# Part of a softmax's row maxima moved from one VectorE reduction per key block to a relu on ScalarE and one fused VectorE pass per two blocks

## The chip, the core and the metric

One of the eight cores of a Trainium2 chip runs the whole kernel. The metric is device time in microseconds (us), the median of a few executions. Beside it stands one execution recorded by the hardware profiler, which gives the start and length of each engine's instructions. The engines are TensorE (PE, with its weight loads as PEld), VectorE (DVE), ScalarE (ACT), GpSimd (POOL) and SyncE (SP, which here issues the DMA transfers). Each works through its own instructions in order and waits on the others only where data or buffers demand it.

## The reference

A block of a transformer in fp32: layer norm, attention with 32 query heads that share one key and one value head, a residual, a second norm, and a feed-forward part with a gated relu.

```python
B, S, D, H = 1, 2048, 512, 32          # Dh = D // H = 16, F = 1792
q = (x @ wq).reshape(B, S, H, Dh).transpose(0, 2, 1, 3)
k = x @ wk
v = x @ wv
scores = einsum("bhqd,bkd->bhqk", q, k) * (Dh ** -0.5)
p = softmax(scores, axis=-1)
o = einsum("bhqk,bkd->bhqd", p, v)
return o.transpose(0, 2, 1, 3).reshape(B, S, H * Dh) @ wo
...
gate = einsum("bsd,df->bsf", x, W_gate)
up = einsum("bsd,df->bsf", x, W_up)
h = gate * (gate > 0) * up
return einsum("bsf,fd->bsd", h, W_down)
...
h = x + A(layernorm(x))
h2 = h + B(layernorm(h))
```

The softmax needs, for each of the 32 heads and each of the 2048 queries, the maximum of 2048 scores. The change is about how these maxima are formed.

## The kernel before

**Precision.** Matmuls run in fp32r, a rounded fp32. Where more is needed, an operand is kept as a rounded part and a remainder, and a product is made of three matmuls (`PASSES`, line 262). GpSimd makes most of these splits: `split_sb` (lines 237 to 241) rounds with a `tensor_scalar` and subtracts with a `tensor_tensor`.

**Units.** The queries are cut into 8 tiles of 256 tokens, and each tile's attention into 4 units of 8 heads: 32 units (`UNITS`). For a unit the queries of its heads lie in one of three buffers `qaug`, the keys of all 2048 tokens in `kaug`. Both hold two copies, in partitions 0 to 63 and 64 to 127; a matmul uses one copy (64 rows of the array), so TensorE runs two lanes beside each other. Letters in lower case mean the lower lane, capitals the upper.

**The maxima (M, m).** `max_mm` (line 612) makes one matmul of 128 queries against a block of 512 keys into a PSUM bank (line 620), and VectorE reduces it to one column of the tile `mpart` (line 622). A unit has 32 steps in each lane: four key blocks j, two halves p, four groups c of 128 queries. `max_finish` (line 624) takes the maximum over the four blocks, splits it, transposes it and sends it through DRAM (`c_dram`) into two further rows of the unit's `qaug`, where it is subtracted by the next matmul.

**The scores (E, e).** `score_mm` (line 653) multiplies 128 keys with 512 queries (line 659); ScalarE takes the exponential out of the bank into a tile `p` (line 662).

**The value blocks (O).** `value_block` (line 666) multiplies the exponentials of 128 keys with the values (line 675), in a bank of its own, "O". All 128 rows are used, so both lanes pause. There are 512 of them, 16 for each unit. `unit_out` (line 690) carries a unit's output away, divides it by its sums on GpSimd and splits it.

**The chains (G, g).** Projections and feed-forward products are chains of matmuls, each in a lower and an upper half (`Chain.half`, line 290, issued at line 297): queries, the output projection of a tile (`front`, line 812), gate and up (`gate_up`, line 853), and down (line 893). When the upper half of a gate chain ends, `hidden` (line 857) issues a relu and a copy on ScalarE (862, 868), the product on GpSimd (870), and then, on GpSimd as well, the splits of the gate and up weights two steps ahead, of the hidden values, and of a down weight, eight instructions. The last tile's gate and up run after all else with the whole array (line 288).

**Banks.** Seven PSUM banks, B0 to B6, go round among maxima, scores, chains and transposes. A bank comes free when VectorE or ScalarE has read it.

**The order.** From line 1033 on, a planner keeps a clock for each lane and engine. What is issued next is written out by hand: `ORDER` is a row of 11,274 letters, and the loop from line 1174 takes one at a time; T stands for transposes and whole matmuls in the first part. `starts` (lines 1209 to 1232) says for each kind when it could start, and the branches from line 1260 issue it and move the planner's clocks with the constants of lines 38 to 42 (`EXP` 494, `RED` 600 ns and so on). These clocks decide when deferred work (splits, loads, residuals) is placed between the letters; instructions go to the engines in the order in which the code issues them. Maxima of a unit may start as soon as its queries are loaded (`qtime`), which needs the scores of the unit three before to be done, and at most one unit ahead of the last finished one.

**Setup.** Key block t comes from `kv(t)` (line 476): `kvt` holds the block unrounded, `kaug` the rounded copy, and its remainder rows are subtracted on VectorE or, for t of 2 and 3, on GpSimd (line 498). The rows of x lie in tiles `xs`: the first 512 tokens in two of the eight `p` tiles, the second in `h`, the third in four tiles `x`, the fourth in four tiles `xn`; later `front` uses two of the `x` and two of the `xn` tiles for each tile of 256 tokens.

Of the kernel before, what the change touches and what calls it, by code (L numbers as in the profile page):

```python
# [8 lines left out]
F32 = mybir.dt.float32  # L9
# [30 lines left out]
EXP, EXP_FREE, RED, RED_FREE, COPY, ADD, FREE = 494, 650, 600, 740, 541, 600, 150  # L40
ROUND, DIFF, PRODUCT, SCALE, HOP, ISSUE = 640, 1290, 1150, 640, 2600, 600
# [8 lines left out]
    "TTTTMMMmMMmmmmmMmTMMmTTTTTMgMggMgmgggMgMggmgmgTTmmTTGmGmGTgMgMgGgMgGGgGgGmggGgGgGGgTTMgMmgGgMGggGgGgMgGgMGmGgG"  # L50
    "gGmgGGmGggGgGgGgGGmMgTmMgGgGgMgGgGGgGmGmGggGgGgMgGgGgGgMGmgGMgGggMGmGGgGggGmGGgGgGmgGgMgGMgGgGmggmGGgGgGggGgMg"
    "MgGgGgMGmGgGmgGgGmGGgGgGmGgGgMgGgGgGgGgGgGgGgMmGgGgGgGgGgGgMgGgGgGgMgGgGmGmGgGgGgGgGmGmMgEgGgGgEgGgMgEgeGGmeGG"
    "mGeGGmGmGmOMeeMeGgGGggMEggMeGgMgEgMgGgEmGGgmMOmEEgmMOMeeGGmeGeGGmeGGmGmGmOmEEgMgEgGggMgEgMgEgMgEgGgGmMmOEmeGeG"
    "GmeGGmGgGgEgMeGgGmEgGgMeGgMgEgGgMgMmOgMeEmMOmEeGmGeGeGGmGgGgMgEgGmEgGmGgGmeGMmOMeEgEgMgOmEmEMeOmEEgMmOeMeMMgOM"
    "geEmMOeMeGGmeGeGGmGeGmGgGgMgEgGgMgEgMgEgMggGEgGmmMOeGGmeGeGmGMmOEmeGeGGmgGGmEgGgMgEgMgEggGgMMmOeMeMgMOeMeEgMMg"
    "OEmEmmMOEmEmOEmeGGmeGeGGmGeGmGEmGeGmGGmMOEeEmMmOMEeEemMOeMmEmEOeMmEEMeOeEeMmEOEemMMeEOeMeEEmMOEeEmeMMOMeEeEmMO"
    "MeEeEMmOeMeEmMOEmEEeeMmMOMeeEEmMOmEEeeMMOMeEeEmMOMmeEeMOmEeeMEEmMOMeeEEMmOEmeEeMMOMmeEmEOMeeMEemEmOeMEmeMEOeME"
    "eEmmOeEmEMeOMEeMmeEOmMEeEmOMeMEEeeMmOEeMmeEmOMmeEEemOEmMeeEmOEmEmeeMOEmeeEmMOeMEmeMEOMemEMEeOMmmEmEeOemeMMEeEm"
    "meMOmMmEEeOMeEmEmOMeMEMmMmeeEOmEMeeMOEmmMMEeEeOmMEeEmOemmMOMmmMMmMEeEeeEMemEOmEeeMEmOMmeEeMOmEmmeeEMmOEmMeEeMm"
    "OeMeMEgEgggMEgMggEgMgMgEggMmOmEeGeGGmeGGmGgGgMgEgMgGgEgMgEgMgGggGmGeGGmmGeGOOmEeGGmeGeGmGeGmGeGGmOMmEmeMOEemEO"  # L60
    "MMeEmeOmMEMMEEeMOmEMeOEmmMmeeOMggEggMggEggMggggEggMggEgggMgOMggMggMmEgGgGgGgGgGeGGgGgEggEggGgGgGmGGeGGmGGeGGgM"
    "ggEggMggGgGgGGmMgeGEgOOmGGeGGmGGeGGmGGeGGmGeGGGMmOEmeGGGgGgMgEggMgggEggMggGgEgGmGgGMeOEmgMgEggMgEgggMgOeMGmGeG"
    "GmGGeGGmGGeGGmGGgGgGgEggGeGGmGGgGgEggMggGgMggEgGgMmOOeMEggEggMggEggMmOeMeGGmGGmGGeGGgGgEggGgMgEggGgMggEggGmGGg"
    "GeGGmGGgGeGmGGgGeMOOmEgMgEggEggMggMmOeGGeGGmGGeGmGGmGGeGGGmGOOmEEegMGgGGgGgMgEgGMgEgMgEgMgGgGmGGeGgGgGmGeGgMgE"
    "gMgEgGgGmMeGgGmEgGgGgGmeMgGggGgeGgGgmGeGgGgGmGeGggOOOEggMggEggMggEggGggMggGmEeGgGgGgGgGeGGmGGgGmGGeGGgMggEggGg"
    "GmGGeGGgGmGGeGOOOemMEggMggEggMgggEggMgOEmeGGmGGeGGgGgGgMggEggGgMgEggGmGgGeGGgMggGEmgGGggGeGGgGgMgEegGgGGgMmOOE"
    "meGGmGGeGGeGGmGGeGGmGGeGGmGGGmGOOMeEggMggEggGgGgMggEggMggEggGgMgEgggEgGMggMOmEeGGmGGeGGeGGmGGeGGmGGeGGmGGGeGGm"
    "GOmMEeGmGOmEeMOeMEgMgEgEggMgEgMgEgMgMggMOOEmeEMgGggGgGmEgGeGgMEggGmGeGgMEgGgMgGmeGGggEggGgeGgGmGgeGmGgGeGmGgmG"
    "eGgGmMgOOMeEggEggMggEgggEggMgOOgMmEeEgGgGgGgGgGgGgMmGgGgGeGgGgMgEggGmGGgGeGgGgMgEggGgGgGgGgGmGGeMeGGmGOOOmEeGG"
    "mGGeGGeGGGmGeGGmGGeGGgGgGgGmGEggGgMggEgggMggMgOOEmeEggMgMgggEggMggOmEeGGmGGeGGmGGeGGmGGeGGgGgGgGmGGeGMggGgGgEg"  # L70
    "gMggGgEggEgGgMmOOMeEggEggMggEggMmOeMmGGeGGmGeGGGmGGeGGmGGeGGmGOeMEmeGGgGGgGGMgEggMgEgEgGEgMgEgMgOOMmEegGGgGmGg"
    "eGgGGmMegGEggMgGEgGggMgGGmEegGgGggGggGmGeGmGeGggMggGmEggGeGmGgOOMemEeMOOmEMggEggMggEggMggEgOeMGmGeGGmGGeGGmGGe"
    "GGmGGeGGmGGGeGGGGmGeEOMmmEMeEOeEmMEeOEmMmEeOMmEeeMOmEMggMEgEggMMgOMeEggGMgEggEgMgGeGmGgEgMgGgGgMmEgGgGeGgEgMgG"
    "gGeGmGeGmOOOeMEggGmEGgMgMggGmGEgGgeGGggGMgmGEeOeGGmeGgGmGeGGmeGGmGemGGmeGOmEeMOEMMEMmEOeEOMemEgMggEgggMgEgggMg"
    "EgggMggEgOMeEmMgggggggMmgeGGgEggGgGgGeGGgmGGmGGgGeGGmGGeGGgGgGmGGeGGgMggEgOOMggEgggMEgggMgEgmMOeEmGGeGGgGgMggG"
    "gEggGGmGeGGgGgMggEggGmGGeGGmGGeGmGGGgeGMgOOmEeMEggEggggMggMgOmEeGGmGGeGGmGGeGGmGGeGGgGgGgMggEggGgGmGGeGMggGgEg"
    "gGgGgMgmEOOeMEggMggEggEggmMOeMeEGmGgGgGgGgGgMgEggGgGmGeGGgMgEggGgGmGeGGgGmGGeGGgGeGGmMOOmEMgEggMggEggeMgOEmeGG"
    "eGGmGGeGGmGGeGGmGGGeGGmGOOMgEggMEggGMgEgMgGgEgEgGMeGgGGmMOOEmeGGmeGeGGmGeGmGgGgMgEgGgMgEgMgEgGgMgMgGmEggGggGge"
    "GgGggGeGmGgeGmGgGeGmGgOOOOgMgEggMggEggEgMggggEmegggMggEggGmGGeGGgMggEggGmGGgGeGGgGmGGeGGmGGgGeGGmGgGeGMgOOmEMg"
    "gEgMggEggeEOeMeGGmGGGmGeGGmGGgGgGgMggEggGgMgEggGgGgGgGmGGeGgGgGmGGOOeMEggMggEggEggmMOeGGmGGeGGmGeGGmGGeGGgGgGg"  # L80
    "MggEggMggGEggMgggGEmgGgGGgeMGggGGgEmGgOMeEmMeOEmeMEggMgOOGmGeGGmGGeGGeGGmGGeGGmGGeGGmGGmEOMeEgEgMgGgGgGMgEgEgM"
    "gEgGgMgMOOEmeGmGgGMggEeGgMgEgGgMgEgGmGeGgMgEmGgGmGeGeGgGggGgMggEggGmGeGggGmGeGmGeGgGmOOOMeEggEggMggEggMggEgggM"
    "OgMgEeGmGgGGggGmGGeGMggGgGmEgGgGgGeGGgGgMgmEgGgGgGeGGmGGgGeMOOmEEegMgEggggMmOeGGeGGmGGeGGmGGeGGmGGmGGgGgGgGeGG"
    "gMggEggGgGgGgMggEggMgEggMggOOEmeMEggMggOmEeEGggMgGgGgGgGmGeGGgGgMgEggGmGeGGmGGgGeGGGgmGGeGGgGgMgmEOOMeEggMggEg"
    "MggEgOmGGeGGeGGmGGeGGmGGeGGmGOOMgEggMEggMGgEgGgGMgEgGgMgGGmGeGGmGgGgEgGgMgEgGgMeGgGmEgGeGgMgEgGmGeGGggMggGmGgm"
# [71 lines left out]
def block_kernel(ctx: ExitStack, tc: tile.TileContext, x, wq, wkv, wo, wgu, wd, out):  # L157
# [924 lines left out]
    def place(k, dep):  # L1082
        return max(lanes[k], issued, dep + LOAD)
# [267 lines left out]
```

## Time and profile before

| what | value |
|---|---|
| median of 3 runs | 1745.73 us (1745.44 to 1750.38) |
| span of the profiled execution | 1747.6 us |
| TensorE: matmul busy, count | 1729.8 us, 15,566 |
| VectorE busy, instructions | 1461.8 us, 2,535 |
| ScalarE busy, instructions | 1252.0 us, 2,487 |
| GpSimd busy, instructions | 848.7 us, 1,004 |
| moved by DMA | 144.07 MB |

Every row of a profile view has the engine, the line of the code, the operation, the output and the inputs by the program's names ("mpart<-B"), their shapes and a count. In the view by groups the numbers behind the bar are the busy time in us, the mean length of one in ns, and the idle time of the engine before them with what ended it. In the timeline a row starts with its start and its length in us, both of the merged group; in the chain of waits likewise. The chain is followed back from the last instruction: at each step to what released it, or to the instruction before it on its engine, so its shares say what set the end. A busy engine is not a limiting one: TensorE's matmuls overlap, and an interval counts once however many run in it.

In the middle of the kernel, in each 200 us, VectorE is busy for about 170 us and GpSimd for about 114:

```profile
600.00:800.00 200.00, 200.00 (x1949) 137.54 (x1943) 170.34 (x295) 146.18 (x291) 117.47 (x140) 1.00 0.27 82
1000.00:1200.00 200.00, 199.88 (x1928) 135.54 (x1927) 168.54 (x290) 145.97 (x290) 114.02 (x137) 1.00 0.27 82
```

(columns: stretch and its length, busy time and count of PE, PEld, DVE, ACT and POOL, granted clock, share and GB/s of DMA).

### The profile page before, as it was taken

How to read it: one execution, taken by the hardware profiler on the slowest of the kernel's cores; microseconds unless marked ns; L12 is line 12 of the kernel's file. 1: busy time of each engine (PE TensorE's matmuls, PEld its weight loads, DVE VectorE, ACT ScalarE, POOL GpSimd, SP SyncE). 2: the span in 40 equal slices, each digit the busy share in tenths (PEclk: the TensorE clock that was granted, in tenths of full speed). 3: DMA queues.
4: the chain of work that ended last, by engine and by line, in shares of the span. 5: the costliest groups of instructions: out<-in, count | busy, mean ns of one | idle time of the engine just before them, and what ended most of it. 6: DMA issues, size and time to landing. Idle time of an engine off the chain costs nothing.

```text
span 1747.6 us, 40171 instructions
## 1 busy us (share of the span) xinstructions
PE 1729.8 (99%) x15566; PEld 1157.3 (66%) x15566; DVE 1461.8 (84%) x2535; ACT 1252.0 (72%) x2487; POOL 848.7 (49%) x1004
## 2 busy tenths in 40 slices
PE   8999999999999999999999999999999999999999
PEld 6864344676656677667666676666667667665788
DVE  8799999888898888988888878988888888885466
ACT  7378987777777777777767767777767777778524
POOL 5422201665527656366626665357546556375510
PEclk9899999999999999999999999999999999999989
DMA  3234111322212222323222222222222223122333
GB/s 128 76 92 114 37 32 31 97 90 78 82 58 92 73 79 77 92 81 96 74 71 88 80 83 77 84 73 83 80 79 90 77 84 95 54 86 68 117 131 116
DMA packets 101970, 144.07 MB, mean 82 GB/s; under 512 B 27156, under 2 KB 39572, under 8 KB 101780
## 3 DMA queue, kind: packets, MB, share of 16 engines
q1 hardware_dynamic: 100724, 141.19, 26.5%
q8 instruction: 122, 2.00, 0.5%
q14 instruction: 68, 0.56, 0.1%
q10 hardware_dynamic: 1056, 0.33, 0.1%
HBM read 119.73 MB, written 21.49 MB: 81 GB/s over the span
## 4 chain that ended last, share of the span: by engine, by line
PE 92%; DVE 7%; DMA 1%; issue 0%; ACT 0%; SPq 0%; POOL 0%; POOLq 0%; ACTq 0%
PE B L297 28%; PE O L675 27%; PE B L620 16%; PE B L659 16%; DVE mpart L622 4%; PE B L288 4%; PE B L515 1%; PE O L927 0%; DMA qaug<-c_dram 0%; PE B L404 0%; DMA c_dram<-mturned 0%; DVE kaug L498 0%; DVE msplit L631 0%; DVE bnst L345 0%; PE B L582 0%
## 5 line engine op out<-in xcount | busy, mean ns | idle before, releaser
L622 DVE TENSOR_REDUCE mpart<-B 128x1 f32<-128x512 f32 x2048 | 1268.5, 682 | 201.0 <-PE B L620 100.4
L662 ACT ACTIVATE p<-B 128x512 f32<-128x512 f32 x2048 | 1091.4, 606 | 358.0 <-PE B L659 194.1
L620 PE MATMUL B<-kaug,qaug 62*128 62x512 f32 x2048 | 760.9, 423 | 6.0 <-DVE hT L567 2.1
L659 PE MATMUL B<-qaug,kaug 64*128 64x512 f32 x2048 | 714.0, 417 | 3.9 <-DMA qaug<-c_dram 3.0
L297 PE MATMUL B<-hn,gu 64*128 64x256 f32 x4704 | 573.8, 281 | 0.0
L297 PEld LDWEIGHTS B<-hn,gu 64*128 64x128 f32 x4704 | 541.6, 186 | 22.1 <-issue 11.6
L675 PE MATMUL O<-p,vv 128*32 128x512 f32 x4096 | 511.4, 601 | 0.0
L620 PEld LDWEIGHTS B<-kaug,qaug 62*128 62x128 f32 x2048 | 353.8, 185 | 159.6 <-DVE mpart L622 49.1
L659 PEld LDWEIGHTS B<-qaug,kaug 64*128 64x128 f32 x2048 | 338.8, 185 | 168.4 <-DVE mpart L622 57.4
L297 PE MATMUL B<-wd,hT 64*128 64x512 f32 x1176 | 273.3, 399 | 0.6 <-DVE wd L247 0.6
L240 POOL TENSOR_TENSOR gu<-wraw,gu 128x512 fp32r<-128x512 f32 x197 | 256.3, 1301 | 16.4
L870 POOL TENSOR_TENSOR hf<-hf,ga 128x256 f32<-128x256 f32 x91 | 66.9, 735 | 398.6 <-ACT hf L868 393.6
L675 PEld LDWEIGHTS O<-p,vv 128*32 128x32 f32 x4096 | 99.7, 108 | 189.8 <-issue 171.1
L297 PEld LDWEIGHTS B<-wd,hT 64*128 64x128 f32 x1176 | 192.6, 187 | 14.4 <-DVE mpart L622 1.9
L239 POOL TENSOR_SCALAR gu<-wraw 128x512 fp32r<-128x512 f32 x197 | 123.3, 626 | 20.5 <-PE B L297 19.4
L240 POOL TENSOR_TENSOR wd<-wraw,wd 128x512 fp32r<-128x512 f32 x91 | 117.5, 1291 | 7.6
L297 PE MATMUL B<-wo,act 64*128 64x512 f32 x384 | 88.5, 393 | 0.0
L725 POOL TENSOR_TENSOR raw<-raw,scale 128x512 f32<-128x512 f32 x15 | 19.3, 1289 | 141.5 <-DMA x<-x 71.6
L862 ACT ACTIVATE ga<-B 128x256 f32<-128x256 f32 x112 | 43.5, 388 | 49.6 <-PE B L288 32.2
L240 POOL TENSOR_TENSOR hT<-hf,hT 128x256 fp32r<-128x256 f32 x94 | 70.4, 749 | 7.8
L297 PEld LDWEIGHTS B<-wo,act 64*128 64x128 f32 x384 | 62.4, 185 | 4.8 <-issue 1.7
L357 POOL TENSOR_TENSOR rs<-ve,nhalf 128x2 f32<-128x2 f32 (+1 forms) x13 | 10.2, 784 | 112.0 <-DVE nm L353 111.9
(139 smaller groups left out, 932.2 us busy)
## 6 DMA issues: line engine op xcount, KB each, us to landing
wraw<-wgu SPq DMA_DIRECT2D x224, 256.0 KB
wraw<-wd SPq DMA_DIRECT2D x112, 256.0 KB
q_dram<-act SPq DMA_DIRECT2D x32, 256.0 KB
qaug<-q_dram SPq DMA_DIRECT2D x62, 128.0 KB
o_dram<-osb SPq DMA_DIRECT2D x31, 256.0 KB
x<-x SPq DMA_DIRECT2D x20, 256.0 KB
out<-h SPq DMA_DIRECT2D x16, 256.0 KB
qaug<-q_dram SPq DMA_DIRECT2D x62, 64.0 KB
```

Source lines behind the costliest of these rows:

```text
L239: nc.gpsimd.tensor_scalar(dst[:, 0], src, 1.0, 0.0, op0=ALU.mult, op1=ALU.add)
L240: nc.gpsimd.tensor_tensor(dst[:, 1], src, dst[:, 0].bitcast(F32), op=ALU.subtract)
L288: nc.tensor.matmul(out(self.bank), l(a), r(b), start=i == 0, stop=i == len(self.ops) - 1)
L297: mm = nc.tensor.matmul(out(self.bank), l(a)[rows], r(b)[rows], start=opens and which == 0, stop=closes and which == 1)
L620: nc.tensor.matmul(b, qaug[v][r, p, c * 128:(c + 1) * 128], kaug[r, j * 512:(j + 1) * 512], start=True, stop=True)
L622: nc.vector.tensor_reduce(mpart[v][:, ab, p, c, j:j + 1], b, axis=AX.X, op=ALU.max)
L659: nc.tensor.matmul(b, kaug[r, kb * 128:(kb + 1) * 128], qaug[v][r, p, :], start=True, stop=True)
L662: nc.scalar.activation(probs[g][:, ab], b, AF.Exp, scale=DH ** -0.5)
L675: nc.tensor.matmul(obank[v][32 * h:32 * h + 32], vv[:, kb, :], probs[g + p][:, ab], start=kb == 0, stop=kb == NB - 1)
L725: nc.gpsimd.tensor_tensor(raw, raw, scale, op=ALU.mult)
L862: nc.scalar.activation(ga[:, :n], p[:, :n], AF.Relu)
L870: nc.gpsimd.tensor_tensor(hf[:, :n], hf[:, :n], ga[:, :n], op=ALU.mult)
```

## The change

For two key blocks with scores a and b, max(a, b) = b + relu(a - b), and a - b is the query times the difference of the two keys. A new letter D (or d) issues the matmul with key differences `kdiff` in place of key block 2, followed by a relu on ScalarE into an SBUF tile; the next maximum in that lane, key block 3, is then reduced by one fused VectorE instruction that adds the relu's tile and takes the maximum along the row. Key block 2's column of `mpart` stays at its start value, so each unit's `mpart` is set to -3e38 first, on GpSimd. The steps of a unit's second half alternate between key blocks 2 and 3; before, block 2's eight steps in each lane came ahead of block 3's. Where no D stands, a maximum is reduced as before.

`kdiff` is made once, on GpSimd, after key block 3. Three `relu` tiles and `kdiff` take the room of four row tiles: `x` and `xn` have two buffers each now in place of four, and xs[2] lies in two more of the `p` tiles. `ORDER` is a new row: 11,268 letters, of them 976 m, 928 M, 48 d, 96 D (1,024 each of m and M before), as many e, E, g, G and O as before, 12 T (18 before).

```diff
+JOINT, APART, RELUS = 640, 2900, 3
...
+    kdiff = consts.tile([128, T], F32R, name="kdiff")
+    lows = consts.tile([128, 1], F32, name="lows")
...
+    nc.gpsimd.memset(kdiff.bitcast(F32), 0.0)
+    nc.gpsimd.memset(lows, 0.0)
+    for b in (32, 96):
+        nc.gpsimd.memset(lows[b:b + 16], -1.0)
...
     def row_tiles(tag, n=4):
-        return [sb.tile([128, D], F32, name=tag, bufs=4) for _ in range(n)]
+        return [sb.tile([128, D], F32, name=tag, bufs=2) for _ in range(n)]
...
-    xs = [[b[:, c] for b in [rows_tile(tag) for _ in range(2)] for c in range(2)] for tag in ("p", "h")]
-    xs += [row_tiles("x"), row_tiles("xn")]
+    xs = [[b[:, c] for b in [rows_tile(tag) for _ in range(2)] for c in range(2)] for tag in ("p", "h", "p")]
+    xs += [row_tiles("x", 2) + row_tiles("xn", 2)]
...
+    def apart(when):
+
+        rows = slice(0, 112)
+        nc.gpsimd.tensor_tensor(kvts[2][rows], kvts[2][rows], kvts[3][rows], op=ALU.subtract)
+        for b in (0, 64):
+            nc.gpsimd.tensor_scalar(kdiff[b:b + 48], kvts[2][b:b + 48], 1.0, 0.0, op0=ALU.mult, op1=ALU.add)
+        for b in (32, 96):
+            nc.gpsimd.tensor_tensor(kdiff[b:b + 16], kvts[2][b:b + 16], kdiff[b:b + 16].bitcast(F32), op=ALU.subtract)
+        stamp["apart"] = on("P", when, APART) + FREE
...
+                if t == 3:
+                    apart(when)
...
-    def max_mm(m, ab, tag):
-
-        v, i = divmod(m, STEPS)
-        j, p, c = i // 8, i // 4 % 2, i % 4
+    def max_step(m):
+
+        i = m % STEPS
+        if i < STEPS // 2:
+            return i // 8, i // 4 % 2, i % 4
+        return 2 + i % 2, (i - STEPS // 2) // 8, (i - STEPS // 2) // 2 % 4
...
+    def max_mm(m, ab, tag, apart=False):
+
+        v = m // STEPS
+        j, p, c = max_step(m)
         if v not in mpart:
             mpart[v] = sb.tile([128, 2, 2, 4, 4], F32, name="mpart", bufs=2)
+            nc.gpsimd.memset(mpart[v], -3e38)
         r = slice(64 * ab, 64 * ab + 62)
         b = bank(tag)
-        nc.tensor.matmul(b, qaug[v][r, p, c * 128:(c + 1) * 128], kaug[r, j * 512:(j + 1) * 512],
-                         start=True, stop=True)
-        nc.vector.tensor_reduce(mpart[v][:, ab, p, c, j:j + 1], b, axis=AX.X, op=ALU.max)
+        keys = kdiff[r] if apart else kaug[r, j * 512:(j + 1) * 512]
+        nc.tensor.matmul(b, qaug[v][r, p, c * 128:(c + 1) * 128], keys, start=True, stop=True)
+        part = mpart[v][:, ab, p, c, j:j + 1]
+        if apart:
+            relus[ab] = sb.tile([128, T], F32, name="relu", bufs=RELUS)
+            nc.scalar.activation(relus[ab], b, AF.Relu)
+        elif ab in relus:
+            over = relus.pop(ab)
+            nc.vector.tensor_tensor_reduce(out=over, in0=b, in1=over, scale=1.0, scalar=-3e38, op0=ALU.add, op1=ALU.max,
+                                           accum_out=part)
+        else:
+            nc.vector.tensor_reduce(part, b, axis=AX.X, op=ALU.max)
...
+                if max_step(w)[0] == 2 and "apart" in stamp:
+                    starts["dD"[k]] = place(k, max(qtime[w // STEPS], bfree[tag], stamp["apart"]))
...
+        elif kind == "D":
+            max_mm(me[k], k, tag, True)
+            lanes[k] = s + PASS
+            slots[k] = len(joined)
+            e0 = max(clk["A"], s + SEEN, joined.get(len(joined) - RELUS, 0.0))
+            joined[slots[k]] = 0.0
+            clk["A"] = e0 + EXP
+            bfree[tag] = e0 + EXP_FREE
+            relu_end[k] = e0 + EXP + 100
+            me[k] += 1
         elif kind == "M":
+            joint = k in relus
             max_mm(me[k], k, tag)
             lanes[k] = s + PASS
-            r0 = max(clk["V"], s + SEEN)
-            clk["V"] = r0 + RED
-            bfree[tag] = r0 + RED_FREE
+            r0 = max(clk["V"], s + SEEN, relu_end.pop(k, 0.0))
+            ns = JOINT if joint else RED
+            clk["V"] = r0 + ns
+            bfree[tag] = r0 + ns + RED_FREE - RED
+            if joint:
+                joined[slots.pop(k)] = clk["V"]
             me[k] += 1
...
```

The rest of the diff is the new row, the dictionary in which the `kvt` tiles are kept, and the planner's use of `key_of`, which names the key block that a step needs. `lows` is not read anywhere.

More of the change, by code (lines that the diff above doesn't have):

```diff
@@ L1042, in block_kernel @@
     exps, oend, qtime = {}, {}, {0: QUERIES_AT}
+    relu_end, joined, slots = {}, {}, {}
     maxed, loaded = 0, 1
@@ L1214, in block_kernel @@
             if w < N and w // STEPS in qtime and w // STEPS <= maxed + 1 and tag and (
[L1215 to L1216 removed]
+                    w >= STEPS or key_of(w) in stamp):
+                starts["mM"[k]] = place(k, max(qtime[w // STEPS], bfree[tag], stamp[key_of(w)] if w < STEPS else 0.0))
+                if max_step(w)[0] == 2 and "apart" in stamp:
+                    starts["dD"[k]] = place(k, max(qtime[w // STEPS], bfree[tag], stamp["apart"]))
             if c is not None and (c.tag or tag):
```

214 lines of the change are left out of this document (108 added, 106 removed).

## The prediction

> **What bounds the kernel now.** I read the page first, then the chain of waits as a whole and cut to two stretches, then the busy time by stretches, then single groups and pieces of the timeline.
>
> ```profile
> span 1747.6 us, 40171 instructions
> PE 1729.8 (99%) x15566; PEld 1157.3 (66%) x15566; DVE 1461.8 (84%) x2535; ACT 1252.0 (72%) x2487; POOL 848.7 (49%) x1004
> ...
> PE 92%; DVE 7%; DMA 1%; issue 0%; ACT 0%; SPq 0%; POOL 0%; POOLq 0%; ACTq 0%
> ```
>
> The last line is the chain by engine: TensorE sets the end for 92% of the span. The 99% busy share says less, since matmuls overlap. VectorE is the only other engine on the chain. The maxima's share of it (line 622) is in these rows: the whole span, the steady middle (400 to 1500 us), and the longest pieces of line 622.
>
> ```profile
> by line: PE B L297 28.1%; PE O L675 26.6%; PE B L620 15.9%; PE B L659 15.6%; DVE mpart L622 4.4%; PE B L288 3.5%; PE B L515 0.7%; PE O L927 0.5%; DMA qaug<-c_dram 0.4%; PE B L404 0.4%; issue 0.4%; DMA c_dram<-mturned 0.3%; DVE kaug L498 0.3
> by line: PE B L297 32.5%; PE O L675 29.9%; PE B L620 17.8%; PE B L659 17.0%; DVE mpart L622 1.5%; PE B L404 0.5%; DVE msplit L631 0.2%; DVE msplit L632 0.2%; issue 0.1%; DVE mfin L627 0.1%; DVE bnst L345 0.1%; DVE mturned L635 0.1%; DVE h L
> 65.67 6.66 DVE mpart L622 x11
> 72.45 13.17 DVE mpart L622 x22
> 272.89 14.38 DVE mpart L622 x24
> 294.63 2.97 DVE mpart L622 x5
> 297.75 4.79 DVE mpart L622 x8
> ```
>
> So 4.4% of 1747.6, or 77 us, of the end hangs on maxima. 1.5% of 1100, 16 us, of it falls in the middle; some 47 us fall in two early stretches (about 65 to 87 and 273 to 303 us), where maxima are late. That 77 us is all that relief of VectorE could give.
>
> ```profile
> 400.00:1500.00 1100.00, 1099.62 (x10497) 739.07 (x10496) 943.94 (x1624) 806.56 (x1599) 618.69 (x736) 1.00 0.26 80
> ```
>
> In the middle (busy: PE, weight loads, VectorE, ScalarE, GpSimd) VectorE is busy for 86%, ScalarE for 73%; the granted clock is 1.00, so the clock has no part in it.
>
> **The change part by part.** First the prices of the instructions it exchanges.
>
> ```profile
> L622 DVE TENSOR_REDUCE mpart<-B 128x1 f32<-128x512 f32 x2048 | 1268.5, 682 | 201.0 <-PE B L620 100.4 <-PE B L659 48.2 <-PE B L297 47.2
> 270.98 17.00 DVE L622 TENSOR_REDUCE mpart<-B 128x1 f32<-128x512 f32 x28 [0.23 <-PE B L620]
> L662 ACT ACTIVATE p<-B 128x512 f32<-128x512 f32 x2048 | 1091.4, 606 | 358.0 <-PE B L659 194.1 <-PE B L620 111.2 <-PE B L297 37.7
> 1646.37 2.06 ACT L662 ACTIVATE p<-B 128x512 f32<-128x512 f32 x4 [0.53 <-PE B L659]
> L823 DVE TENSOR_TENSOR h<-B,x 128x512 f32<-128x512 f32 x16 | 10.9, 680 | 3.0 <-PE B L297 3.0
> L351 DVE TENSOR_SCALAR ve<-mv 128x2 f32<-128x2 f32 (+1 forms) x12 | 2.1, 176 | 0.1
> ```
>
> Back to back, 28 maxima take 17.00 us: (17.00 - 0.68)/27 = 0.60 us a step. Four exponentials take 2.06 us: (2.06 - 0.61)/3 = 0.48 us a step. The new row has 144 letters D or d (96 and 48). Each turns two 0.60 us maxima into a relu on ScalarE and one fused pass. I give the relu an exponential's 0.48 us (same shape, also out of PSUM). The fused pass the trace does not show. It can't cost less than a maximum, 0.60; the nearest row is line 823 (PSUM and SBUF in, 0.68 alone, as long as a maximum alone); the upper end adds a small VectorE instruction for the reduced column, 0.68 + 0.18 = 0.86. I take 0.66, near line 823. A pair then leaves VectorE 1.20 - 0.66 = 0.54 us, 144 of them 78 us (between 49 and 86), and puts 144 x 0.48 = 69 us on ScalarE. TensorE does as many matmuls of the same size as before: no gain there.
>
> [...]
>
> What of the 78 us reaches the end? In the first unit 10 pairs (5.4 us) stand against the new order, which wants key block 3 as early as block 2, and five GpSimd instructions more (1.3 us each for the subtractions, as the splits in the rows further down) before the key differences exist: -2. Around the second stretch (values 64 to 96 of the 512) the new row has 172 maxima, 30 of them paired at the cost of 142 VectorE passes; the old row has 146. VectorE is loaded the same there, but 26 maxima are ahead for later: -4. In the middle half of its 16 us: -8. Together **-14**. The rest of the 78 us lies beside TensorE's work and gives nothing.
>
> The new row also groups the value blocks (letter O) otherwise: 311 runs of O against 341.
>
> ```profile
> 910.15 0.50 PE L659 MATMUL B<-qaug,kaug 64*128 64x512 f32 x2
> 910.58 1.07 PE L675 MATMUL O<-p,vv 128*32 128x512 f32 x8
> 911.58 0.50 PE L620 MATMUL B<-kaug,qaug 62*128 62x512 f32 x1
> 363.69 2.72 PE O L675 x24
> 676.53 3.57 PE O L675 x32
> 1649.06 0.12 PE B L659
> ```
>
> A block inside a run takes 3.57 - 2.72 = 0.85 us, and a score matmul a slot of 0.12. The lone block above starts 0.43 us after the first of two score matmuls (0.19 over two slots), and the next work comes 1.00 us later (0.15 over 0.85): a change to O and back costs 0.34 us. 30 fewer: **-10**. This term needs no relief of VectorE.
>
> The tail: 138 instead of 195 chain halves (g, G) are left after the last O.
>
> ```profile
> 1649.65 1.92 PE O L675 x16
> 1655.24 13.29 PE B L297 x109
> 1675.02 7.53 PE B L297 x20
> 1682.55 61.22 PE B L288 x420
> 1675.61 1.41 DVE L397 TENSOR_TENSOR hn<-B,hn 128x256 fp32r<-128x256 f32 x4
> ```
>
> The last tile's inputs are ready at 1675.61 + 1.41 = 1677.0; TensorE is still on older halves until 1682.5, some at 0.38 us each since one lane is alone. With 57 fewer, those 5.5 us go, perhaps 3 more from an undisturbed norm; the 57 halves cost 57 x 0.09 = 5 us where they go now: **-3** (0 to -8).
>
> Against this, each of the 32 units now has a memset of its maxima's tile on GpSimd, issued ahead of its first maximum. It is short (128x64, a quarter of line 941's 0.32 us tile below), but GpSimd runs in order, and VectorE is in order too: behind a late memset wait the unit's first maximum, all maxima after it, the splits and residual sums of VectorE, and TensorE once no bank is free. So I laid the issue order of the code against the trace. Two units of the old order, and that memset:
>
> ```profile
> L941 POOL MEMSET p<- 128x256 f32 x4 | 1.1, 318 | 0.0
> 163.49 4.94 DVE L622 TENSOR_REDUCE mpart<-B 128x1 f32<-128x512 f32 x8
> 172.35 1.30 POOL L240 TENSOR_TENSOR wo<-wraw,wo 128x512 fp32r<-128x512 f32 x1
> ...
> 1446.67 0.62 POOL L239 TENSOR_SCALAR gu<-wraw 128x512 fp32r<-128x512 f32 x1
> 1452.54 1.29 POOL L240 TENSOR_TENSOR wd<-wraw,wd 128x512 fp32r<-128x512 f32 x1
> 1446.81 1.89 DVE L622 TENSOR_REDUCE mpart<-B 128x1 f32<-128x512 f32 x3 [0.21 <-PE B L659]
> ```
>
> Unit 29's first maximum is the third of the three at 1446.81, at 1448.0. The splits issued ahead of it, down to the wd one, end at 1453.83: a memset there would have held VectorE 5.8 us. Unit 3's is the seventh of the group at 163.49, at 167.2, against 173.65 on GpSimd (the split at 172.35): 6.5 us. In 17 of the 32 units the excess is positive, first unit 3, last unit 29, 64 us in all. In the old row the units that begin within 5 us (counted in slots) of a gate chain's end, whose splits are GpSimd's burst, have 3.8 us on average; those that begin over 7.5 us after it have almost none. Of units 7 to 31 the old row begins 14 within 5 us; the new row begins 7, and 18 at 8.8 us or later. So 7 x 3.8 and unit 3's 6.5 give 33 us of held VectorE. Seven banks, some three of them with exponentials and chains, take in the maxima of about 2.5 us (four, at 0.60 us and more apart) before TensorE stops; 3.8 - 2.5 = 1.3, and something for the queue behind: 1.5 us in 8 units, **+12** (0 if the banks take it all, 33 if they take nothing).
>
> Small ones: a relu holds its bank on ScalarE at 78% instead of 73% busy and the fused pass waits for it, **+2** (0 to 8). Halving the row buffers, loading xs[2] into p tiles and zeroing kdiff cost nothing as long as the loads run ahead behind the previous tile's chains, some 200 us; without that cover one load per tile would show. Relu and Exp share a table: the group view has one table load in all, with relus among the exponentials now.
>
> ```profile
> L949 ACT ACT_TABLE_LOAD x1 | 1.3, 1283 | 1.8 <-issue 1.8
> ```
>
> **Sum**: -14 - 10 - 3 + 12 + 2 = -13 us against the profiled 1747.6, which lies 1.9 above the median of the runs, 1745.73. Forecast 1745.7 - 13 = 1733 us; its own range, with tail and memset at their ends (-5 - 12, +3 + 21), is 1716 to 1757.
>
> **The rivals.**
> First, slower: the memset decides. Its place is the first maximum of a unit, its price what the banks don't take in. Against: the new row begins most units clear of the bursts. For: the 17 excesses above, with GpSimd busy for 56% of the middle (619 of 1100 us). If the new row's timing drifts by a few us against its letters, it meets the bursts as the old row would: 64 us of held VectorE, of which 0.65 goes to the end, 42, against gains of 27: 1745.7 - 27 + 2 + 42 = 1763. It turns the sign once more than 25 us come through, 0.8 us per unit. Chance 0.18.
> Second, the pairs give nothing: TensorE is 92% of the chain, 97% in the middle by its four lines. Then grouping, tail, memset and small ones are left: -10 - 3 + 12 + 2 = +1, so 1747; with a memset that hides, 1735. Middle 1741. Chance 0.2.
> Third, relief counts more than by its share, since maxima far ahead leave banks free for scores: half of the 77 us: -38 - 13 + 4 (the memset hidden), 1699. For: 201 us of line 622's own idle time show that its queue is often empty, so it is bursts of maxima that block, and a pair shortens a burst. Against: the middle's 1.5%. Chance 0.12.
> Fourth, the change doesn't relieve VectorE at all: a fused pass of 1.2 us, two steps of a maximum, gives -10 - 3 + 12 + 10 for relus and waits: 1755. Against: line 823, with the same operands, takes 0.68. Chance 0.06.
>
> **How the numbers follow.** The forecast has 0.44. A measurement of this kernel tells about 0.3% (5.2 us) from no change: faster is below 1740.5, slower above 1751. Faster: 0.38 of the forecast, 0.1 of the second, 0.12 of the third: 0.60. Same: 0.05 of the forecast, 0.07 of the second, 0.03 of the first and 0.02 of the fourth: 0.17. Slower: the rest, 0.23. The range takes in the first rival's middle and most of the way to the third: 1706 to 1763.
>
> **What would show it.** Per pair a fused row of 0.6 to 0.9 us alone and a relu of 0.6 on ScalarE; 1904 VectorE passes on maxima; VectorE 70 to 80 us less busy, ScalarE 85 more (144 x 0.606). The share of VectorE on the chain down from 7% to about 6, with a new entry for waits on the memset's line in the waits view of some 20 to 40 us. L675's value blocks in 311 runs. Block L288 starting within 2 us of line 397's end. It is wrong if the memset's waits exceed 50 us, if a fused row takes over 1 us, or if the gain sits in the middle on VectorE's share by more than 16 us.

## The result, and the profile after

The changed kernel takes 1772.03 us (median of 4 runs, 1770.07 to 1774.4) beside 1746.55 us for the kernel before on the same chip: 1.0141 times as long, 95% interval 1.0126 to 1.0157. It is slower by 25 us; 1733 was forecast, and 1772 lies above the range.

The page of the changed kernel: span, busy time by engine, and the chain of waits by engine and line.

```profile
span 1768.3 us, 40468 instructions
PE 1707.0 (97%) x15566; PEld 1153.7 (65%) x15566; DVE 1388.4 (79%) x2546; ACT 1299.8 (74%) x2628; POOL 844.4 (48%) x1034
...
PE 77%; POOL 12%; issue 6%; DVE 2%; DMA 1%; ACT 1%; SPq 0%; POOLq 0%; ACTq 0%; DVEq 0%
PE B L304 24%; PE O L718 23%; PE B L702 15%; PE B L655 11%; POOL gu L247 4%; PE B L295 3%; POOL wd L247 2%; POOL gu L246 2%; DVE mpart L665 1%; POOL hT L247 1%; POOL hf L913 1%; POOL wd L246 1%; PE B L536 1%; POOL hT L246 1%; PE O L970 0%
```

Before, GpSimd had 0% of the chain and VectorE 7%. Now GpSimd has 12%, with the splits of weights and of hT (lines 246 and 247), which no maximum reads; VectorE is down to 2%. So VectorE was relieved, and the time went to a place where TensorE waits for GpSimd. The groups of instructions by line (busy us, mean ns of one, then the idle time before them and what ended it) say through what:

```profile
L665 DVE TENSOR_REDUCE mpart<-B 128x1 f32<-128x512 f32 x1760 | 1101.1, 683 | 251.1 <-PE B L655 150.0 <-POOL mpart L651 49.8 <-PE B L702 30.9
L662 DVE CUSTOM_DVE_ANT_0 relu<-B,relu 128x512 f32<-128x512 f32 x144 | 96.7, 685 | 21.4 <-PE B L655 7.3 <-ACT relu L659 5.2 <-PE B L304 5.0
L662 DVE DVE_READ_ACCUMULATOR2_ANT mpart<- 128x1 f32 x144 | 12.0, 83 | 0.0
L659 ACT ACTIVATE relu<-B 128x512 f32<-128x512 f32 x144 | 84.8, 605 | 23.9 <-PE B L655 23.2
L651 POOL MEMSET mpart<- 128x64 f32 x32 | 4.8, 151 | 2.7 <-DVE mfin L670 2.7
```

The maxima (line 665) stood 49.8 us behind the memset of their own tile, line 651, which itself takes 0.15 us. The view of waits (us in all, times, longest) gives the number of stops, and what stood behind VectorE:

```profile
DVE mpart L665 <- POOL mpart L651: 49.8, 10, 8.6
PEld B L702 <- DVE mpart L665: 69.0, 66, 7.4
PEld B L655 <- DVE mpart L665: 38.4, 24, 7.4
```

One stop in full, the start of unit 18, from the timelines of four engines (start, duration, engine, line, count, and in brackets the idle time before and what ended it):

```profile
876.65 0.73 POOL L913 TENSOR_TENSOR hf<-hf,ga 128x256 f32<-128x256 f32 x1 [4.28 <-DMA wraw<-wgu]
...
883.12 1.26 POOL L247 TENSOR_TENSOR wd<-wraw,wd 128x512 fp32r<-128x512 f32 x1
884.32 0.15 POOL L651 MEMSET mpart<- 128x64 f32 x1
```
```profile
872.86 3.15 DVE L665 TENSOR_REDUCE mpart<-B 128x1 f32<-128x512 f32 x5 [0.30 <-PE B L655]
884.51 1.29 DVE L665 TENSOR_REDUCE mpart<-B 128x1 f32<-128x512 f32 x2 [8.49 <-POOL mpart L651]
```
```profile
876.19 0.39 ACT L911 ACTIVATE hf<-B 128x256 f32<-128x256 f32 x1
```
```profile
876.01 1.92 PE L718 MATMUL O<-p,vv 128*32 128x512 f32 x16
...
878.20 0.39 PE L304 MATMUL B<-wd,hT 64*128 64x512 f32 x1
885.25 0.79 PE L702 MATMUL B<-qaug,kaug 64*128 64x512 f32 x1 [6.67 <-DVE mpart L665]
```

GpSimd starts the product of a gate chain at 876.65. The view puts the wait before it down to a weight load, but ScalarE's copy of `hf`, which the product reads, ends only at 876.19 + 0.39 = 876.58. GpSimd then works through eight instructions of splits, and the memset comes behind all of them, in order. VectorE ends its last maximum at 876.01 and stands for 8.49 us. TensorE goes on for 2.2 us, most of it a value block, whose matmuls take no new bank, and then starts nothing from 878.20 to 885.25. A matmul of the same shape that took 0.39 us before the stop takes 0.79 right after it. The busy time by stretches around this stop (PE, weight loads, VectorE, ScalarE, GpSimd, then the granted clock, DMA share, GB/s):

```profile
870.20:878.20 8.00, 8.00 (x75) 5.15 (x73) 5.51 (x9) 6.48 (x14) 3.55 (x6) 1.00 0.48 149
878.20:885.25 7.05, 0.39 (x3) 0.00 (x0) 0.74 (x2) 0.60 (x1) 6.02 (x8) 0.82 0.00 0
885.25:889.25 4.00, 4.00 (x18) 3.90 (x20) 3.07 (x6) 1.69 (x4) 0.00 (x0) 0.50 0.13 38
889.25:893.25 4.00, 4.00 (x37) 2.95 (x38) 3.69 (x7) 3.79 (x8) 0.94 (x1) 0.97 0.35 99
```

So a stop costs twice: the 7.05 us in which nothing starts, and then some 4 us at a granted clock of 0.50, with 18 matmuls where the next 4 us have 37 (some of them the shorter ones of a value block). There are seven stops of this kind, at units 7, 8, 18, 21, 24, 25 and 26. Their stretches together:

```profile
sum 42.60, PE 2.91 PEld 0.26 DVE 5.67 ACT 5.80 POOL 35.47; mean PE 0.42 PEld 0.04 DVE 0.81 ACT 0.83 POOL 5.07
```

Before, no two successive matmul starts were more than 2.3 us apart. After each of the seven stops the clock was at half for 3.4 to 6.1 us; added up in steps of half a microsecond (step times one minus the clock) that loses 15 us. 42.6 + 15 = 58 us.

### The profile page after: what moved, and what is told of

It reads as the page before. It is cut to its first block, busy times and chain, and to the rows that moved or that the text cites. A ratio compares the mean times of both kernels' runs of the same rounds, so it can differ in the third digit from the quotient of the medians.

```text
span 1768.3 us, 40468 instructions
## 1 busy us (share of the span) xinstructions
PE 1707.0 (97%) x15566; PEld 1153.7 (65%) x15566; DVE 1388.4 (79%) x2546; ACT 1299.8 (74%) x2628; POOL 844.4 (48%) x1034
## 4 chain that ended last, share of the span: by engine, by line
PE 77%; POOL 12%; issue 6%; DVE 2%; DMA 1%; ACT 1%; SPq 0%; POOLq 0%; ACTq 0%; DVEq 0%
PE B L304 24%; PE O L718 23%; PE B L702 15%; PE B L655 11%; POOL gu L247 4%; PE B L295 3%; POOL wd L247 2%; POOL gu L246 2%; DVE mpart L665 1%; POOL hT L247 1%; POOL hf L913 1%; POOL wd L246 1%; PE B L536 1%; POOL hT L246 1%; PE O L970 0%
## 5 line engine op out<-in xcount | busy, mean ns | idle before, releaser
L705 ACT ACTIVATE p<-B 128x512 f32<-128x512 f32 x2048 | 1067.8, 613 | 337.8 <-PE B L655 193.5
L665 DVE TENSOR_REDUCE mpart<-B 128x1 f32<-128x512 f32 x1760 | 1101.1, 683 | 251.1 <-PE B L655 150.0
L655 PE MATMUL B<-kaug,qaug 62*128 62x512 f32 x1904 | 714.7, 422 | 28.8 <-DVE mpart L665 23.9
L655 PEld LDWEIGHTS B<-kaug,qaug 62*128 62x128 f32 x1904 | 333.8, 186 | 89.0 <-DVE mpart L665 37.4
L304 PE MATMUL B<-wd,hT 64*128 64x512 f32 x1176 | 295.4, 402 | 0.1
L247 POOL TENSOR_TENSOR gu<-wraw,gu 128x512 fp32r<-128x512 f32 x191 | 247.7, 1297 | 15.9
L246 POOL TENSOR_SCALAR gu<-wraw 128x512 fp32r<-128x512 f32 x191 | 118.4, 620 | 25.3 <-PE B L304 24.8
L662 DVE CUSTOM_DVE_ANT_0 relu<-B,relu 128x512 f32<-128x512 f32 x144 | 96.7, 685 | 21.4 <-PE B L655 7.3
L659 ACT ACTIVATE relu<-B 128x512 f32<-128x512 f32 x144 | 84.8, 605 | 23.9 <-PE B L655 23.2
```

The source lines that it names most:

```text
L246: nc.gpsimd.tensor_scalar(dst[:, 0], src, 1.0, 0.0, op0=ALU.mult, op1=ALU.add)
L247: nc.gpsimd.tensor_tensor(dst[:, 1], src, dst[:, 0].bitcast(F32), op=ALU.subtract)
L304: mm = nc.tensor.matmul(out(self.bank), l(a)[rows], r(b)[rows], start=opens and which == 0, stop=closes and which == 1)
L655: nc.tensor.matmul(b, qaug[v][r, p, c * 128:(c + 1) * 128], keys, start=True, stop=True)
L659: nc.scalar.activation(relus[ab], b, AF.Relu)
L662: nc.vector.tensor_tensor_reduce(out=over, in0=b, in1=over, scale=1.0, scalar=-3e38, op0=ALU.add, op1=ALU.max, accum_out=part)
```

## The experiments

Times are medians; "before" is the kernel before, measured beside them on the same chip (1750.0, 1748.9 and 1749.0 us). Theory: the late memset costs some 60 us and the rest of the change gains.

**The memset on VectorE.**

```diff
-            nc.gpsimd.memset(mpart[v], -3e38)
+            nc.vector.memset(mpart[v], -3e38)
```

> The changed kernel with the memset of each unit's maxima on VectorE instead of GpSimd, nothing else. Theory (GpSimd's queue ahead of the memset is what costs): the 10 waits on the memset (49.8 us) and the seven stops of TensorE behind them (42.6 us) are gone, 32 VectorE memsets of about 0.1 us are added: 1725 to 1732 us, faster than before. Rival (the new row or the pairs cost the time, and the memset only shows where the slack is): TensorE stops at the same places for another reason and the time stays above 1755 us.

1716.96 us, ratio 0.9824 (0.9802 to 0.9846). With the one word changed the kernel is faster than before, by more than was expected (1725 to 1732 us).

**The memset on GpSimd, one unit earlier.** Three tiles instead of two, and the next unit's tile is set at the current unit's start.

```diff
-        if v not in mpart:
-            mpart[v] = sb.tile([128, 2, 2, 4, 4], F32, name="mpart", bufs=2)
-            nc.gpsimd.memset(mpart[v], -3e38)
+        while len(made) <= min(v + 1, len(UNITS) - 1):
+            mpart[len(made)] = sb.tile([128, 2, 2, 4, 4], F32, name="mpart", bufs=3)
+            nc.gpsimd.memset(mpart[len(made)], -3e38)
+            made.append(v)
```

> The changed kernel with the memset left on GpSimd but issued one unit earlier (three buffers instead of two for the maxima's tile). If the price is the queue ahead of the memset and not GpSimd's memset as such, it has a whole unit of some 50 us to be done: 1723 to 1731 us, like the VectorE memset version or a little faster. If GpSimd's memset itself disturbs VectorE, it stays above 1750 us.

1711.35 us, ratio 0.9792 (0.9772 to 0.9812): the lowest median here, below the 1723 to 1731 expected; two kernels further down, at 1712.0 and 1712.8, are level with it within the noise. Its chain by engine, and the group of maxima:

```profile
PE 96%; DVE 2%; POOL 1%; issue 1%; DMA 0%; ACT 0%; POOLq 0%; SPq 0%; DVEq 0%; ACTq 0%
...
L666 DVE TENSOR_REDUCE mpart<-B 128x1 f32<-128x512 f32 x1760 | 1100.3, 683 | 193.6 <-PE B L656 147.4 <-PE B L703 31.0 <-PE B L304 10.4
```

The wait on the memset is gone from the maxima's idle time (251.1 to 193.6, of which 49.8 is that wait), and GpSimd's share of the chain falls from 12% to 1%. 1772.0 - 1711.4 = 61 us is what the place of the memset cost; between the two profiled spans it is 1768.3 - 1711.6 = 57, beside the 58 counted from stops and clock.

**Four late memsets.** As the last kernel, but the memsets of units 7, 8, 18 and 21 are issued where the change has them.

```diff
+            if len(made) not in (7, 8, 18, 21):
+                nc.gpsimd.memset(mpart[len(made)], -3e38)
...
+        if v in (7, 8, 18, 21) and v not in late:
+            nc.gpsimd.memset(mpart[v], -3e38)
```

> The new row with pairs, the memset one unit ahead for all units but 7, 8, 18 and 21, where it stands ahead of the unit's first maximum as in the change; there VectorE was held 7.5, 7.8, 8.5 and 8.6 us. It measures what a held microsecond costs. Theory (a bank is named when the matmul is issued, so TensorE stops at the first matmul whose named bank waits for VectorE, and a restart costs more): 32 us held cost 28 to 40 us, 1739 to 1751 us. Rival (the prediction's price: free banks take in about 2.5 us per unit): 22 us or less, 1733 us or below.

1749.48 us, ratio 1.0009 (0.9999 to 1.0018): four instructions of 0.15 us take 38 us. The view of waits:

```profile
DVE mpart L670 <- POOL mpart L655: 32.7, 4, 8.7
```

TensorE starts nothing for 7.44, 7.60, 7.11 and 6.72 us, 28.9 in all, and the half clock after them loses 9.5: 38.4 us (34 between the two profiled spans). For each us held, 34 / 32.7 to 38 / 32.7, 1.05 to 1.17 us, reach the end; in the changed kernel it is 57 / 49.8 to 61 / 49.8, 1.14 to 1.22.

**The old row with the memset alone.** The kernel before, unchanged but for a memset that nothing in it needs.

```diff
             mpart[v] = sb.tile([128, 2, 2, 4, 4], F32, name="mpart", bufs=2)
+            nc.gpsimd.memset(mpart[v], -3e38)
```

> The kernel before with only the memset of each unit's maxima on GpSimd added, ahead of the unit's first maximum (it changes no result, since every column is written). Theory: the trace of before had 17 units whose GpSimd work ended after that maximum, 64 us in all; with about 1.5 us per unit taken in by the banks, some 35 to 40 us reach the end: 1775 to 1790 us. Rival (a held VectorE is taken in by banks and by work of other engines, as the prediction priced it, or the memset hurts only in the new row): 1746 to 1755 us.

1859.6 us, ratio 1.0637 (1.061 to 1.0664), far beyond what was expected. The view of waits:

```profile
DVE mpart L623 <- POOL mpart L618: 93.4, 19, 8.5
```

The prediction had read 64 us in 17 units for this row out of the trace of before; it is 93.4 in 19. The price is 110 / 93.4 = 1.17 us for each us held, as in the new row.

**The new row without pairs.** Each D is an ordinary maximum of key block 2: no key differences, relus, fused passes or memset; the row and the planner's clocks stay.

```diff
-        keys = kdiff[r] if apart else kaug[r, j * 512:(j + 1) * 512]
+        keys = kaug[r, j * 512:(j + 1) * 512]
...
-            relus[ab] = sb.tile([128, T], F32, name="relu", bufs=RELUS)
-            nc.scalar.activation(relus[ab], b, AF.Relu)
+            relus[ab] = None
```

> The changed kernel's row of letters with each D issued as an ordinary maximum of key block 2: no key differences, no relus, no fused passes, no memset; the planner's clocks are left as they are. It tells the row from the pairs. Theory (grouping of value blocks and the shorter tail are worth about 15 us, the pairs another 10 to 15): 1730 to 1745 us, slower than the VectorE memset version by 5 to 20 us. Rival (pairs give nothing because TensorE sets the pace): the same as the VectorE memset version within 3 us.

1772.31 us, ratio 1.014 (1.0119 to 1.016): slower than before, where 1730 to 1745 was expected. Its chain by engine, and the chain by line in the middle (400 to 1500 us) of this kernel, then of the one with the memset ahead:

```profile
PE 81%; DVE 17%; issue 1%; DMA 1%; ACT 0%; POOL 0%; SPq 0%; POOLq 0%; ACTq 0%; DVEq 0%
by line: PE O L707 28.2%; PE B L304 25.5%; PE B L691 17.2%; DVE mpart L654 14.3%; PE B L648 12.9%; DVE h L926 0.5%; PE B L411 0.5%; issue 0.4%; DVE msplit L663 0.2%; DVE msplit L664 0.1%; DVE bnst L352 0.1%; DVE h L855 0.1%; DVE mfin L659 0
```
```profile
by line: PE B L304 33.8%; PE O L719 30.1%; PE B L703 19.0%; PE B L656 15.3%; DVE mpart L666 0.7%; PE B L411 0.6%; DVE msplit L675 0.2%; DVE relu L663 0.1%; DVE msplit L676 0.1%; issue 0.1%; DVE mfin L671 0.0%; DVE mturned L679 0.0%; DVE sum
```

The maxima have 14.3% of the middle's chain in the new row without pairs, 1.5% in the old row, 0.7% in the new row with them. The new row asks VectorE for maxima earlier than it can deliver them one by one. Within this row the pairs are worth 1772.3 - 1711.4 = 61 us, or 0.42 us each, with the planner's clocks, which count on the pairs, left as they are.

**Half the pairs.** Every second pair made ordinary, memset ahead.

```diff
+            pairs_seen.append(m)
+            plain = len(pairs_seen) % 2 == 0
```

> The new row with the memset one unit ahead, and every second pair issued as two ordinary maxima. With all pairs it took 1711.4 us, with none 1772.3. Theory (each pair takes about 0.42 us off a VectorE that sets the pace of this row): half way, 1738 to 1746 us. Rival (only bursts count, and half of the pairs clear most of them): 1715 to 1730 us.

1742.9 us, ratio 0.9972 (0.9962 to 0.9983). 72 pairs are worth 1772.3 - 1742.9 = 29 us, the other 72 are worth 32: near enough linear.

**The first unit without pairs.**

```diff
+            plain = m < STEPS
```

> The new row with the memset one unit ahead and the pairs of unit 0 alone issued as ordinary maxima. TensorE stops 3.7 us before the first matmul with key differences, which GpSimd has not made yet. Theory: that stop goes, but VectorE gets 10 more passes of 0.6 us where maxima are late: between 1708 and 1714 us, no clear gain. Rival (the key differences are what delays the whole beginning): 1706 us or less.

1712.81 us, ratio 0.9801 (0.9782 to 0.9819), beside 0.9792 with them: no difference that can be told. The forecast's gain in the first unit (-2) is not there.

**The old row with pairs.** 135 pairs in even steps over units 2 to 28, memset ahead. From unit 1 on the second half of a unit's steps has to alternate between key blocks 2 and 3.

```diff
+            if 2 <= w // STEPS < 29 and i >= 0 and i % 2 == 0 and (i // 2 + int(letter.isupper())) % 3 == 0:
+                letter = "dD"[int(letter.isupper())]
```

> The row of letters of before with 135 of its maxima of key block 2, spread evenly over units 2 to 28, formed in pairs, and the memset on GpSimd one unit ahead. It tells whether pairs help a row that wasn't made for them. Theory (VectorE's queue holds TensorE's banks in bursts, and each pair shortens a burst): the prediction's share of the pairs, some 10 to 20 us, shows here too: 1725 to 1738 us. Rival (the pairs pay only in the new row, whose maxima run as far ahead as queries allow; here ScalarE's extra 65 us collide with exponentials): 1742 us or more.

1783.99 us, ratio 1.0206 (1.0186 to 1.0225): 35 us slower than before. The groups of its fused passes:

```profile
L663 DVE CUSTOM_DVE_ANT_0 relu<-B,relu 128x512 f32<-128x512 f32 x135 | 93.1, 690 | 101.8 <-ACT relu L660 54.1 <-PE B L656 17.5 <-PE B L703 14.0
```

Here VectorE stands 54.1 us behind relus, against 5.2 in the changed kernel. That looked like the cause, and was put to the test by taking the pairs out again:

```diff
         if apart:
-            relus[ab] = sb.tile([128, T], F32, name="relu", bufs=RELUS)
-            nc.scalar.activation(relus[ab], b, AF.Relu)
-        elif ab in relus:
+            relus[ab] = None
```

> The kernel of the old row with spread pairs, with each D again an ordinary maximum of key block 2 (no relus, no fused passes; the step order, the memset a unit ahead and the planner's clocks stay). It took 1784 us with its pairs, 35 more than the kernel before. Theory (the pairs cost it, since VectorE stands 54 us behind relus that come too late in this row): without them about the time before, 1742 to 1756 us. Rival (the other order of the steps, or the planner's changed clocks, cost it): 1770 us or more.

1773.92 us, ratio 1.0142 (1.0128 to 1.0156). The theory falls: 25 of the 35 us come without any pair, and the pairs and their waits add 10. Not all of the 25 is the order of the steps. The first value block of this run already starts 6.6 us later than before, and one row of its view of waits shows a part of that, at the first maximum of unit 0, whose memset can't be issued a unit ahead:

```profile
DVE mpart L662 <- POOL mpart L651: 3.7, 1, 3.7
```

The rest grows over the whole kernel. The other order of the steps, the planner's changed clocks and the halved row buffers weren't tried apart. In this row VectorE's relief gains nothing that its waits don't take back.

**The memset ahead, on VectorE.** Asked because the memset on VectorE at the old place (1716.96) and on GpSimd a unit ahead (1711.35) lie 5.6 us apart.

> As the memset a unit ahead with three tiles (1711.4 us), but on VectorE. The memset on VectorE with two tiles at the old place took 1717.0 us. Theory (the 5.6 us between them are VectorE's own 32 memsets, 3.6 us busy, in the way of maxima): 1714 to 1720 us. Rival (the third tile and the earlier place are what helps): 1708 to 1713 us, no more than on GpSimd.

1712.03 us (one of five runs 1717.05), ratio 0.9798 (0.9783 to 0.9812). VectorE's 32 memsets are not what costs. The interval overlaps with that of the memset on VectorE at the old place (0.9802 to 0.9846), so whether the third tile gains the rest, or nothing is left to explain, stays open.

## Why the prediction was wrong

**The step that failed is the price of the memset**, +12 in the sum, 61 measured. Its mechanism was predicted and its places too: seven units of 7 to 31 within 5 us of a gate chain's end, and unit 3. It named no unit, but in the trace with the memset ahead seven of these units begin from 0.5 us before to 4.5 us after a gate chain's end (taken as the start of the relu that reads it), and they are the seven that stopped TensorE; three more (28 to 30) begin 0.9 to 1.5 us ahead of one, and the rest over 8 us after one. Unit 3 held VectorE for 3.0 us. Both factors of the price were too small.

First, the time held: 33 us were worked out, 49.8 measured. A unit's 3.8 us on average, read from where the splits stood against the first maximum in the old row, became 45.6 / 7 = 6.5. The old row itself, with the memset alone, gives 93.4 where 64 had been read. The reading fell short by a factor of 1.5 in both rows. What it missed, in the main, is the place of a unit's first maximum. It took unit 29's to be the third of the three at 1446.81, which is the first behind 29 x 64 maxima. But the two lanes run apart, and one begins the next unit while the other is still on the last. In the run of the old row with the memset alone, the same three maxima stand behind the memset together:

```profile
1552.48 1.89 DVE L623 TENSOR_REDUCE mpart<-B 128x1 f32<-128x512 f32 x3 [7.20 <-POOL mpart L618]
```

So the first of the three is unit 29's, and the reading should have been 1453.83 - 1446.81 = 7.0 us, not 5.8; 7.2 were measured. In all 19 units held in that run, the maximum that waits stands up to three places earlier than a count of 64 for each unit says, as the letters of `ORDER` have it. From these places the trace of before gives 91 us, beside 93.4 measured, and for the 14 of units 7 to 31 that were held over 1 us it gives 6.1 us each; 7 x 6.1 is 43, beside the 45.6 of the new row. Unit 3, read at 6.5 us in the old row, wasn't held there at all.

Second, what reaches the end: it was set at 1.5 of 3.8 us, because banks would take in 2.5 us of maxima. The seven stops are 42.6 of the 45.6 us held: banks and value blocks take in, net, 0.4 us a unit. Why is read from the code, not from the trace: a score matmul's bank is named when the code is issued, so the author takes TensorE to stop at the first matmul whose bank still holds an unread maximum, even if others are free. The trace shows that the matmul which ends unit 18's stop is a score and waited for VectorE (the row at 885.25, 6.67 us); how many banks were free then wasn't counted. On top of that comes the half clock, which the prediction did not have at all. At 1.17 us for each us held, even the 33 us that it had worked out would have cost 39 us instead of 12, and the forecast would have been 1760.

The first rival, that the memset decides, is what happened, though not on its condition: the timing didn't drift against the letters, the bursts were met where the forecast had them. Its 1763 was 64 us held at 0.65; it was 50 held at 1.22, so that its time comes near is in part luck. The wait on the memset's line, 49.8 us, lies beyond the 20 to 40 named and just under the 50 named as what would refute the forecast. VectorE's share of the chain fell to 2%, not 6.

**The pairs** (-14). Their prices were right: a fused row 0.685 us alone (0.6 to 0.9 named), 1904 passes, VectorE 73 us less busy (70 to 80 named); neighbouring fused passes start 0.612 us apart by their median, a maximum behind a fused pass 0.616, maxima 0.598, so 0.66 was a little high. Behind each fused pass stands a second row, `DVE_READ_ACCUMULATOR2_ANT`, of 83 ns, where the prediction's upper end had put 0.18 us; but the step is less than 0.02 us longer than a maximum's. ScalarE is 48 us busier, not 85: the relus take 84.8, but the exponentials 1067.8 instead of 1091.4, more of them back to back (1702 of the 2048 start before ScalarE's instruction ahead of them has ended, 1471 before), and relus overlap with them too (107 of the 144 start so). The +2 for relus that come late holds: 5.2 us of waits.

What failed in that step is its ceiling, "77 us is all that relief of VectorE could give". It treats the new row as the old one with fewer maxima. In the new row the pairs carry 61 us, because that row without them waits for VectorE (17% of its chain) and takes 1772; in the old row, with its steps in the other order, they cost 10. Row and pairs are one change, and neither part has a price of its own.

**The rest of the sum**, by the kernel with the memset ahead against before (1711.6 - 1747.6 = -36 in span; -25 was forecast without the memset). The time between value blocks, less 0.115 us for each score matmul and 512-wide half, 0.059 for each 256-wide one and 0.855 for each value block, leaves the changes to O and TensorE's stalls. Changes: 311 runs for 341, counted at the forecast's 0.34 us each, -10. Stalls to the 64th value block: +5 (forecast -2), of which 3.7 us is one gap right before the first matmul with key differences. From the 64th to the 96th: 12.4 to 4.7 us, -8 (forecast -4). Behind that: 55 to 38 us, -17 (forecast -8). The tail after the last O is 11.8 us shorter, with 5 us of its halves done earlier: -7 (forecast -3, 0 to -8). The clock has a part in that. The prediction read the old tail's halves of 0.38 us as one lane alone, but the granted clock there was 0.50, and it stayed so from 1674.8 to 1685.0:

```profile
1674.80:1682.50 7.70, 7.48 (x22) 5.15 (x22) 2.88 (x7) 0.00 (x0) 0.00 (x0) 0.50 0.09 34
```

That loses up to 5.1 us by the same count as for the stops; in the tail with the memset ahead both slices of 42.8 us on the page show a clock of 0.9 or more, where the page of before shows 0.8 in the 43.7 us around that stretch. The last block of line 295 starts within 1 us of line 404's end of its inputs, as said. Two small figures of the prediction are off and change nothing: the rows of line 622 in the two early stretches add up to 45 us (with one of 2.7 us that it does not show), not 47, and 144 relus of 0.606 us are 87 us, not 85. So the gains were there, and larger than forecast; the memset alone turned the sign.

## What to carry to other kernels

Before a small instruction goes onto an engine that runs in order (as GpSimd here: 0.15 us of memset came behind eight splits, and VectorE stood for 8.49 us), ask what may stand ahead of it in the worst unit, which of its readers comes first in either lane, and who is next behind that reader; issue it a unit early, or on the engine that reads its result. Price a stop of the engine that sets the end at its full length and add the slow clock after it (here 42.6 us and 15); before counting buffers as cover, ask whether the next instruction can take whichever is free (here banks and value blocks took in 0.4 of 6.5 us a unit). A row written for a new instruction mix can be worse without that mix than the row it replaces (here 1772 us beside 1750), so test the parts of such a change together with the row, not in the old one.

## What the runs showed of the hardware that was not expected

In the changed kernel TensorE's granted clock falls to half at each of the seven stops. Unit 18's stop was shown; here are the 4 us from about the end of the six others (columns as above; the third number from the right is the clock):

```profile
343.00:347.00 4.00, 4.00 (x20) 1.80 (x22) 2.33 (x5) 1.19 (x3) 0.00 (x0) 0.53 0.00 0
389.40:393.40 4.00, 3.98 (x18) 1.08 (x22) 2.53 (x6) 0.00 (x0) 0.00 (x0) 0.50 0.04 6
1042.30:1046.30 4.00, 4.00 (x18) 3.54 (x20) 3.81 (x10) 1.69 (x3) 0.00 (x0) 0.50 0.05 9
1196.70:1200.70 4.00, 3.99 (x23) 2.16 (x26) 3.69 (x7) 1.19 (x2) 0.00 (x0) 0.58 0.00 0
1250.80:1254.80 4.00, 4.00 (x20) 1.57 (x24) 3.63 (x7) 0.00 (x0) 0.00 (x0) 0.57 0.16 37
1306.60:1310.60 4.00, 3.90 (x18) 1.90 (x22) 3.33 (x8) 1.57 (x3) 0.00 (x0) 0.50 0.13 23
```

The shortest of these stops is 3.7 us, the longest 7.5; half clock lasts 3.4 to 6.1 us after them and loses 1.7 to 3.0 us each. These 15 us fill the gap between the 42.6 us in which TensorE started nothing and the 57 by which the spans differ.

Whether the clock falls does not go by the length of a stop alone in these runs. The old row with the memset alone has a stop of 3.51 us with the clock at 1.00 in it and behind it (first two rows). The changed kernel is at half behind a stop of 2.07 us that ends at 161.34 (third row), and the old tail shown above is at half with no two matmul starts more than 2.3 us apart.

```profile
1280.77:1284.28 3.51, 0.28 (x6) 0.07 (x3) 0.75 (x2) 0.59 (x2) 2.64 (x4) 1.00 0.23 75
1284.28:1287.70 3.42, 3.42 (x36) 2.29 (x37) 3.28 (x9) 2.83 (x6) 0.47 (x1) 1.00 0.03 5
162.00:166.00 4.00, 4.00 (x23) 1.18 (x22) 3.32 (x7) 2.08 (x4) 0.00 (x0) 0.57 0.14 39
```

So the clock stayed at 1.00 through a stop of 3.51 us, and was at half behind one of 2.07 us and behind no such stop. What sets it in these places was not shown.
